# A norm of tokens moved from VectorE to ScalarE, and two differences of h made in one operation

## The chip, the cores and the metric

The kernel runs on one core of a Trainium2 chip. The metric is device microseconds of one execution: the median of three runs before the change, and the same after it. Lower is better.

## The reference

Two layers are applied twice to x of 2048 tokens by 576 features. `_A_ref` is attention with 32 heads of 18, each token looking at 8 keys at distance 0, 2, ..., 14; `_B_ref` is a feed-forward part of width 4608 with SiLU. Each gets a normalised x (mean and variance over the 576 features, no weights).

```python
def _layernorm(x, axis=-1, eps=1e-5):
    m = jnp.mean(x, axis=axis, keepdims=True)
    v = jnp.var(x, axis=axis, keepdims=True)
    return (x - m) / jnp.sqrt(v + eps)
...
    def _B_ref(x, w1, w2):
        h = jnp.einsum("bsd,df->bsf", x, w1)
        h = _silu(h)
        out = jnp.einsum("bsf,fd->bsd", h, w2)
        return out

    x = A_x
    x = x + _A_ref(_layernorm(x, axis=-1), A_wqkv, A_wo)
    x = x + _B_ref(_layernorm(x, axis=-1), B_w1, B_w2)
    x = x + _A_ref(_layernorm(x, axis=-1), A_wqkv, A_wo)
    x = x + _B_ref(_layernorm(x, axis=-1), B_w1, B_w2)
    return x
```

## The kernel before

Everything is float32 in and out; a factor of a matrix product is split into two float16 parts (a high one, and the rest), and three products of parts stand for one. The tokens are taken in chunks of 512 (four tiles of 128 tokens, `NJ`), four chunks for each of the two rounds, so that there are eight steps s = 0 to 7. A step is: attention (`attention`), projection (`project`), norm, feed-forward. Attention runs on VectorE (products, sums, softmax) after a qkv product on TensorE; the feed-forward is nearly all TensorE.

In steps 0 and 1 the feed-forward is done plainly (`ffn`). From step 2 on it is done by block products (`ffn_pairs`): the four 2x2 blocks of a product are made from seven products P1 to P7 of sums and differences of blocks. The forms of the tokens are made in `forms`, called once for each of the steps 2 to 7. It takes the mean and variance of each of the four tiles (bn_stats, lines 1162 and 1163), an inverse square root by Newton's method for all four (`newton`, lines 530 to 539, thirteen small operations on 128x4), then normalises each tile by one VectorE operation that subtracts the mean and multiplies (line 1179), and makes four differences for each of the two halves a of the tokens (line 1184). Each of the seven forms is then split into a high part (ScalarE, line 1193) and a low part (VectorE, line 1198) and turned by a DMA transpose that SP issues (line 1203) into a tile xf, of which there are nine. These are the right sides of the products of line 1232. In steps 2 and 3 the normalised tiles go into areas of their own (`home`), in steps 4 to 7 they are written over x.

Of the feed-forward's other side, the pairs q = 0 to 17 of each step: seven products into PSUM banks, ScalarE copies (`snap`, line 1236), VectorE additions (line 1239), SiLU on ScalarE (lines 1256 to 1261). In steps 6 and 7 (`TWICE`) the second product is by block products too, and `hidden_forms` makes three more forms of h from rows of a tile hq with seven rows of 128x256: row 4 = 6 + 3, row 5 = 4 - 0, row 2 = 1 - 5, row 6 = 0 - 6 (line 1286), and then splits rows 0 to 2 and 3 to 6 into high and low parts (ScalarE line 1291, VectorE line 1294). `seconds` multiplies them (line 1322) and adds the result to x (line 1331). In steps 2 to 5 the second product is line 1345, and line 1353 takes its five banks out.

The order of the work is not written out by hand. Each operation is handed to a planner (`Plan`) by `op`, with an engine, an estimated duration, the keys it reads and writes, and a priority. `Plan.order` plays time forward: whenever an engine is free in its model, the ready operation of lowest priority number and then of lowest number in the program starts, if its buffers are free. The result is one list, and each engine, and each queue that issues DMAs, works through its part of it strictly in that order on the chip. The planner looks at nothing that lies ahead of its clock. The estimates are in the code: 2.55 us for `newton`, 0.58 for a normalisation, 0.42 for a difference of h. ScalarE's table loads are modelled for operations that name a table (exp, silu).

Of the kernel before, what the change touches and what calls it, by code (L numbers as in the profile page):

```python
# [13 lines left out]
AF = mybir.ActivationFunctionType  # L14
ALU = mybir.AluOpType
AX = mybir.AxisListType

P = 128
# [8 lines left out]
NJ = 4  # L27
# [17 lines left out]
LNX = 512.0  # L45
# [29 lines left out]
class Plan:  # L75
# [18 lines left out]
    def op(self, eng, dur, fn, reads=(), writes=(), prio=0.0, nbytes=0, table=None, after=(), lanes=1, lag=0.0):  # L94
        o = Op()
        o.lag = lag
        o.eng, o.dur, o.fn, o.prio, o.seq, o.nbytes, o.table = eng, dur, fn, prio, len(self.ops), nbytes, table
        o.outs, o.end, o.lanes = [], None, lanes
        deps = set(after)
        for k in reads:  # L100
            if k in self.writer:
                deps.add(self.writer[k])
        for k in writes:
            if k in self.writer:
                deps.add(self.writer[k])
            deps.update(self.readers.get(k, ()))
        for k in reads:
            self.readers.setdefault(k, []).append(o)
        for k in writes:
            self.writer[k] = o  # L110
            self.readers[k] = []
        deps.discard(o)
        o.deps = deps
        o.n = len(deps)
        for d in deps:
            d.outs.append(o)
        o.bufs = []
        for k in (*reads, *writes):
            b = k[0] if isinstance(k, tuple) else k
            if isinstance(b, Buf) and b not in o.bufs:  # L120
                o.bufs.append(b)
                b.left += 1
                if b.turn is None:
                    b.turn = self.named[b.tag]
                    self.named[b.tag] += 1
        self.ops.append(o)
        return o
# [152 lines left out]
def sliding_attention_silu_ffn(ctx: ExitStack, tc: tile.TileContext, x, wqkv, wo, w1, w2, out):  # L280
    nc = tc.nc
# [5 lines left out]
    op = S.op  # L287
# [11 lines left out]
    def T(b):  # L299
        if isinstance(b, tuple):  # L300
            return T(b[0])[:, b[1]]
        return S.tags[b.tag][b.slot]
# [221 lines left out]
    def newton(st, mv, nt, on_act, unit, js=slice(0, NJ)):  # L524

        v, r, a, b = (T(nt)[:, i, js] for i in (0, 1, 3, 4))
        if on_act == 2:
            nc.vector.tensor_scalar(v, T(st)[:, js, 0, 1], 1.0 / D, EPS, op0=ALU.mult, op1=ALU.add)
        else:
            nc.vector.tensor_scalar(v, T(mv)[:, js, 1], EPS, None, op0=ALU.add)  # L530
        nc.vector.tensor_scalar(a.bitcast(I32), v.bitcast(I32), 1, None, op0=ALU.logical_shift_right)
        nc.vector.tensor_scalar(r.bitcast(I32), a.bitcast(I32), -1, 0x5F3759DF, op0=ALU.mult, op1=ALU.add)
        for s in (1.0, unit):

            nc.vector.tensor_tensor(a, r, r, op=ALU.mult)
            nc.vector.tensor_tensor(a, a, v, op=ALU.mult)
            nc.vector.tensor_scalar(b, a, 0.375 * s, -1.25 * s, op0=ALU.mult, op1=ALU.add)
            nc.vector.tensor_tensor(b, b, a, op=ALU.mult)
            nc.vector.scalar_tensor_tensor(r, b, 1.875 * s, r, op0=ALU.add, op1=ALU.mult)
        if on_act in (1, 3):  # L540
            nc.vector.tensor_scalar(T(nt)[:, 2, js], T(mv)[:, js, 0], -1.0, None, op0=ALU.mult)

# [613 lines left out]
    def forms(xs, prio, home=None, late=(), into=None):  # L1156

        st, mv, nt = Buf("st"), Buf("mv"), Buf("nt")
        for j in range(NJ):
            def stats(j=j):  # L1160
                for h in range(2):
                    nc.vector.bn_stats(T(st)[:, j, h, :], T(xs[j])[:, h * KH:(h + 1) * KH])
                nc.vector.bn_aggr(T(mv)[:, j, :], T(st)[:, j])
            op("DVE", 0.99, stats, [xs[j]], [(st, j), (mv, j)], prio)
        op("DVE", 2.55, lambda: newton(st, mv, nt, False, LNX), [(st, j) for j in range(NJ)] + [(mv, j) for j in range(NJ)], [nt], prio)
        out, ys = {}, [Buf(home[0]), Buf(home[1])] if home else [Buf(into)] * 2

        def view(a, r):
            if home:
                return T(ys[a])[:, r]  # L1170
            if r > 3:
                return T(ys[a])[:, a, r - 4]
            return T(xs[a + 2 - r // 2 * 2])[:, r % 2 * KH:(r % 2 + 1) * KH]

        def key(a, r):
            return (ys[a], r) if home else (ys[a], a, r) if r > 3 else xs[a + 2 - r // 2 * 2]
        for a in range(2):
            for j, r in ((a + 2, 0), (a, 2)):
                op("DVE", 0.58, lambda a=a, j=j, r=r: nc.vector.tensor_scalar(
                    T(ys[a])[:, r:r + 2, :].rearrange("p a b -> p (a b)") if home else T(xs[j]), T(xs[j]), T(mv)[:, j, 0:1], T(nt)[:, 1, j:j + 1],  # L1180
                    op0=ALU.subtract, op1=ALU.mult), [xs[j], (mv, j), nt], [key(a, r), key(a, r + 1)], prio)

            for o, u, v in ((4, 0, 2), (5, 1, 4), (6, 1, 0), (7, 3, 5)):
                op("DVE", 0.45, lambda a=a, o=o, u=u, v=v: nc.vector.tensor_tensor(view(a, o), view(a, u), view(a, v), op=ALU.subtract),
                   [key(a, u), key(a, v)], [key(a, o)], prio, after=late)
        for n in P_ORDER:
            r, x = Y_ROW[n], Buf("xf")
            for a in range(2):
                f = Buf("yf")

                def hi(f=f, a=a, r=r):
                    d, y = T(f), view(a, r)
                    nc.scalar.activation(d[:, 0:KH], y, AF.Copy)
                    nc.scalar.activation(d[:, KH:KH + 32], y[:, 2 * P:KH], AF.Copy)

                def lo(f=f, a=a, r=r):
                    d, y = T(f), view(a, r)
                    nc.vector.tensor_tensor(d[:, 3 * P:KB], y[:, 0:2 * P], d[:, 0:2 * P], op=ALU.subtract)
                    nc.vector.tensor_tensor(d[:, KH + 32:3 * P].rearrange("p (a b) -> p a b", a=2), y[:, None, 2 * P:KH].to_broadcast([P, 2, 32]),
                                            d[:, None, 2 * P:KH].to_broadcast([P, 2, 32]), op=ALU.subtract)  # L1200
                op("ACT", 0.65, hi, [key(a, r)], [(f, 0)] if home else [(f, 0), (x, "hold", a)], prio)
                done = op("DVE", 0.64, lo, [key(a, r), (f, 0)], [(f, 1)], prio)
                op("SP", 1.34, lambda f=f, a=a, x=x: nc.sync.dma_start_transpose(T(x)[:, :, a * P:(a + 1) * P], T(f)),
                   [(f, 0), (f, 1)], [(x, a)], prio, nbytes=P * KB * 4)
            out[n] = x
        formed.append(done)
        return out

    def ffn_pairs(s, xf, xs, first):
# [3 lines left out]
        for g, n in enumerate(G2):  # L1213
# [4 lines left out]
            for q in range(q0, q0 + n):  # L1218
# [44 lines left out]
                if twice:  # L1263
                    hidden_forms(q, hq, h, pd)
                    continue
# [16 lines left out]

    def hidden_forms(q, hq, h, pd):

        for r, u, v, o in ((4, 6, 3, ALU.add), (5, 4, 0, ALU.subtract), (2, 1, 5, ALU.subtract), (6, 0, 6, ALU.subtract)):
            op("DVE", 0.42, lambda hq=hq, r=r, u=u, v=v, o=o: nc.vector.tensor_tensor(T(hq)[:, r], T(hq)[:, u], T(hq)[:, v], op=o),
               [(hq, u), (hq, v)], [(hq, r)], pd - 0.01)
        for r0, r1, sh in ((0, 3, shx), (3, 7, shy)):
            sc = sh[:, q:q + 1]
            m = (r1 - r0) * 2 * P  # L1290
            op("ACT", 0.3 + m / 1200, lambda hq=hq, h=h, sc=sc, r0=r0, r1=r1: nc.scalar.activation(
                flat_rows(T(h)[:, 0, r0:r1]), flat_rows(T(hq)[:, r0:r1]), AF.Copy, scale=sc),
               [(hq, r) for r in range(r0, r1)] + ["wsc"], [(h, r0)], pd)
            op("DVE", 0.22 + m / 960, lambda hq=hq, h=h, sc=sc, r0=r0, r1=r1: nc.vector.scalar_tensor_tensor(
                flat_rows(T(h)[:, 1, r0:r1]), flat_rows(T(hq)[:, r0:r1]), sc, flat_rows(T(h)[:, 0, r0:r1]),
                op0=ALU.mult, op1=ALU.subtract), [(hq, r) for r in range(r0, r1)] + [(h, r0)], [(h, r0)], pd)

    def flat_rows(t):
        return t.rearrange("p a b -> p (a b)")
# [217 lines left out]
    def turn(s):  # L1517
        XT[s] = forms(load_x(s, s - 1.0, spilt=True), s - 1.0, into="ye")
        X[s] = load_x(s, s - 1.0, spilt=True)
# [73 lines left out]
```

## Time and profile before

| | us |
|---|---|
| median of three runs | 2123.3 (2121.58 to 2124.65) |
| the profiled execution, as a run | 2119.38 |
| its span, first to last instruction | 2117.6 |
| TensorE busy | 2088.3 |
| VectorE busy | 1754.9 |
| ScalarE busy | 1025.8 |
| GpSimd busy | 388.5 |

The mean granted TensorE clock is 0.998 of full. The profile gives instructions by line of the kernel, by engine and by the program's tile names (buffer numbers left out); tiles that share an area carry the area's name, so hq appears as `wq` or `w`, and the forms' tiles as `wos`, `o`, `prs` and `x`. A matmul's end is modelled, and since matmuls are pipelined the shown durations of neighbours overlap: what one really takes is read from the starts, or from a piece of many. "Idle before" is the time that an engine sat still before an instruction, with the instruction that ended the wait.

### The profile page before, as it was taken

To read this page: it belongs to the slowest core of one execution; us is meant where nothing else is said; L and a number is where in the kernel's file an instruction comes from. 1 tells how busy PE (TensorE), PEld (TensorE's weight loads), DVE (VectorE), ACT (ScalarE), POOL (GpSimd) and SP (SyncE) were. 2 spreads that over 40 slices of the span, in tenths; PEclk is the share of its full clock that TensorE was granted. 3 is DMA by queue.
4 is the path that set the end of the run, shared out by engine and by line. 5 is a ranking of instruction groups with operands and counts; after the bars stand their busy time and mean duration, and the time that the engine had idled before them with its cause. 6 is when DMAs were issued, how large, how long until landed. Compare 5 with 4: busy or idle time off the path is not lost.

```text
span 2117.6 us, 41751 instructions
## 1 busy us (share of the span) xinstructions
PE 2088.3 (99%) x16017; PEld 1539.5 (73%) x16017; DVE 1754.9 (83%) x2861; ACT 1025.8 (48%) x1857; POOL 388.5 (18%) x628
## 2 busy tenths in 40 slices
PE   8999999999999999999999999999999999999999
PEld 4556556665566888877786777777788888888887
DVE  8899999999876998679997978986996748766665
ACT  7555787644345454434434433434444545444442
POOL 2133566343322232011111001001000000000000
PEclk9999999999999999999999999999999999999999
DMA  6477777687989889886677896786989999779772
GB/s 188 146 212 256 236 258 248 214 243 221 250 206 297 264 275 252 210 261 189 177 220 208 218 273 195 217 225 185 247 256 302 330 258 290 218 213 272 221 210 76
DMA packets 377632, 489.07 MB, mean 231 GB/s; under 512 B 150600, under 2 KB 300724, under 8 KB 373080
## 3 DMA queue, kind: packets, MB, share of 16 engines
q1 hardware_dynamic: 332456, 336.85, 56.9%
q0 software_dynamic: 42960, 148.45, 21.8%
q8 instruction: 125, 2.05, 0.4%
q10 hardware_dynamic: 2016, 1.11, 0.2%
q14 instruction: 75, 0.61, 0.1%
HBM read 350.96 MB, written 86.85 MB: 207 GB/s over the span
## 4 chain that ended last, share of the span: by engine, by line
PE 87%; DVE 6%; DMA 4%; ACT 1%; issue 1%; SPq 0%; POOL 0%; ACTq 0%; DVEq 0%
PE acc L1345 19%; PE z L1232 16%; PE misc L1232 10%; PE z L735 9%; PE acc L1322 9%; PE z L1385 7%; PE acc L1409 4%; PE misc L1345 4%; PE misc L735 3%; PE z L925 3%; PE misc L1385 2%; PE misc L925 1%; DMA kvs<-kvs 1%; DMA yo<-yh 1%; DVE prs L837 1%
## 5 line engine op out<-in xcount | busy, mean ns | idle before, releaser
L1232 PEld LDWEIGHTS <-w 128*128 128x128 f16 x5292 | 516.5, 98 | 74.5 <-issue 2.5
L1345 PE MATMUL acc<-w,h 128*128 128x320 f16 (+2 forms) x3780 | 548.2, 280 | 2.3 <-DVE x L1353 2.3
L1345 PEld LDWEIGHTS <-h 128*128 128x128 f16 x4320 | 407.6, 98 | 122.3 <-issue 3.3
L1232 PE MATMUL z<-xb,w 128*128 128x256 f16 x3213 | 405.0, 273 | 0.5 <-DVE wq L1239 0.5
L1232 PE MATMUL misc<-xb,w 128*128 128x256 f16 x2079 | 272.2, 273 | 1.1 <-DVE wq L1239 0.8
L735 PEld LDWEIGHTS <-xa 128*128 128x128 f16 x1344 | 130.8, 98 | 115.5 <-issue 6.7
L837 DVE TENSOR_TENSOR prs<-qts,kvs 128x2304 f32<-128x2304 f32 x64 | 163.4, 2554 | 18.8 <-DMA kvs<-kvs 17.0
L870 DVE TENSOR_TENSOR prs<-kvs,pe 128x1152 f32<-128x1152 f32 x128 | 170.3, 1352 | 1.0
L841 DVE TENSOR_REDUCE lg<-prs 128x128 f32<-128x2304 f32 x64 | 163.1, 2548 | 0.9
L735 PE MATMUL z<-wq,xa 128*128 128x432 f16 x840 | 160.2, 346 | 2.1 <-ACT h L748 2.1
L1345 PE MATMUL misc<-w,h 128*128 128x384 f16 x540 | 139.7, 326 | 0.0
L877 DVE TENSOR_TENSOR prs<-prs 128x1152 f32<-128x1152 f32 (+1 forms) x128 | 135.1, 1056 | 3.2
L1331 DVE SCALAR_TENSOR_TENSOR x<-acc,d2x,x 128x576 f32<-128x576 f32 (+1 forms) x85 | 68.7, 810 | 57.2 <-PE acc L1322 56.6
L1385 PEld LDWEIGHTS <-w 128*128 128x128 f16 x588 | 57.9, 99 | 74.2 <-issue 7.6
L1409 PE MATMUL acc<-w,h 128*128 128x288 f16 x864 | 108.4, 286 | 1.9 <-DVE h L1392 1.1
L1409 PEld LDWEIGHTS <-h 128*128 128x128 f16 x864 | 83.7, 98 | 25.2 <-DVE h L1392 1.4
L1385 PE MATMUL z<-xb,w 128*128 128x512 f16 x420 | 93.9, 379 | 0.7 <-DVE w L1011 0.6
L1385 PE MATMUL z<-xb,wq 128*128 128x512 f16 x420 | 92.8, 379 | 1.7 <-ACT h L1387 1.7
L1236 ACT ACTIVATE wq<-z 128x256 f32<-128x256 f32 x107 | 40.8, 382 | 103.8 <-PE z L1232 103.7
L1387 ACT ACTIVATE h<-z,d 128x512 f32<-128x512 f32 x60 | 40.9, 682 | 94.9 <-PE z L1385 86.4
L1322 PEld LDWEIGHTS <-h 128*128 128x128 f16 x756 | 74.0, 98 | 17.6
L925 PEld LDWEIGHTS <-yo 128*128 128x128 f16 x672 | 65.7, 98 | 18.6 <-issue 1.9
(322 smaller groups left out, 3369.0 us busy)
## 6 DMA issues: line engine op xcount, KB each, us to landing
w<-wfs SPq DMA_DIRECT2D x756, 160.0 KB, 3.9
w<-w2s SPq DMA_DIRECT2D x180, 288.0 KB, 4.9
wq<-wqs SPq DMA_DIRECT2D x17, 1080.0 KB, 6.6
kvs<-kd POOLq DMA_DIRECT2D x8, 1584.0 KB, 8.4
w<-w1s SPq DMA_DIRECT2D x36, 320.0 KB, 5.9
wfs<-xa POOLq DMA_DIRECT2D x18, 640.0 KB, 4.6
kvs<-wts SPq DMA_DIRECT2D x80, 144.0 KB, 3.1
w2s<-w POOLq DMA_DIRECT2D x36, 288.0 KB, 4.7
```

The lines of the kernel that those rows point to most:

```text
L735: nc.tensor.matmul(T(m)[:, :3 * UC], a, b, start=n == 0, stop=n == len(pl) - 1)
L837: nc.vector.tensor_tensor(T(pr), T(qt)[:, j:j + 2, None, :].to_broadcast([P, 2, W, UC]), win(T(kv), j, 2), op=ALU.mult)
L841: nc.vector.tensor_reduce(T(lg)[:, j:j + 2].rearrange("p a w h -> p (a w h)"), T(pr).rearrange("p a w (h d) -> p (a w h) d", d=DH), axis=A ...
L870: nc.vector.tensor_tensor(T(pr)[:, a].rearrange("p w (h d) -> p w h d", d=DH), v, T(pe)[:, j + a, :, :, None].to_broadcast([P, W, UH, DH]) ...
L877: nc.vector.tensor_tensor(t[:, :, 0:h, :], t[:, :, 0:h, :], t[:, :, h:2 * h, :], op=ALU.add)
L925: nc.tensor.matmul(T(m)[:, 0:288], a, b, start=n == 0, stop=n == len(pl) - 1)
L1232: nc.tensor.matmul(t, w[:, u, :], v[:, r, :], start=first and m == 0, stop=m == 6, skip_group_check=True)
L1322: nc.tensor.matmul(T(acc)[:, j, 0:KH], T(hb[t])[:, a, row[k], j * P:(j + 1) * P], T(wb[k, t])[:, w, :], start=k in (5, 1, 2) and t == 0 an ...
L1331: nc.vector.scalar_tensor_tensor(v, T(acc)[:, a:b, 0:KH], d2x[:, g:g + 1], v, op0=ALU.mult, op1=ALU.add)
L1345: nc.tensor.matmul(T(fa[b])[:, o:o + 2 * n].rearrange("p (a b) -> p a b", a=2), h(f, a, j), w(f)[:, :, v, c:c + n], start=q == f == m == 0 ...
L1385: nc.tensor.matmul(T(z), v, u, start=m == 0, stop=m == len(pl) - 1)
L1409: nc.tensor.matmul(T(acc)[:, h, 0:288], T(hb[q])[:, a, j * P:(j + 1) * P], T(wbs[q][0])[:, h, w, :], start=q == 0 and m == 0, stop=q == n ...
```

## The change

In `forms`, the four tiles of a step are normalised by ScalarE instead of VectorE: x * r + (-mean * r), an Identity activation with scale and bias read per token. `newton` gets a mode 4 for it, with one more operation that makes -mean * r for the four tiles; the planner's estimate for `newton` stays at 2.55 us, and the normalisation is handed to it as 0.7 us of ScalarE. In `hidden_forms`, rows 5 and 6 are made by one VectorE operation over two rows: its first operand steps backwards from row 4 to row 0, its second forwards from row 0 to row 6. Four operations become three, in the order 4, (5 and 6), 2.

```diff
@@ newton
+        if on_act == 4:
+            nc.vector.scalar_tensor_tensor(T(nt)[:, 2, js], T(mv)[:, js, 0], -1.0, r, op0=ALU.mult, op1=ALU.mult)
         if on_act in (1, 3):
             nc.vector.tensor_scalar(T(nt)[:, 2, js], T(mv)[:, js, 0], -1.0, None, op0=ALU.mult)
@@ forms
-        op("DVE", 2.55, lambda: newton(st, mv, nt, False, LNX), [(st, j) for j in range(NJ)] + [(mv, j) for j in range(NJ)], [nt], prio)
+        op("DVE", 2.55, lambda: newton(st, mv, nt, 4, LNX), [(st, j) for j in range(NJ)] + [(mv, j) for j in range(NJ)], [nt], prio)
@@ forms
-                op("DVE", 0.58, lambda a=a, j=j, r=r: nc.vector.tensor_scalar(
-                    T(ys[a])[:, r:r + 2, :].rearrange("p a b -> p (a b)") if home else T(xs[j]), T(xs[j]), T(mv)[:, j, 0:1], T(nt)[:, 1, j:j + 1],
-                    op0=ALU.subtract, op1=ALU.mult), [xs[j], (mv, j), nt], [key(a, r), key(a, r + 1)], prio)
+                op("ACT", 0.7, lambda a=a, j=j, r=r: nc.scalar.activation(
+                    T(ys[a])[:, r:r + 2, :].rearrange("p a b -> p (a b)") if home else T(xs[j]), T(xs[j]), AF.Identity,
+                    bias=T(nt)[:, 2, j:j + 1], scale=T(nt)[:, 1, j:j + 1]), [xs[j], (mv, j), nt], [key(a, r), key(a, r + 1)], prio)
@@ hidden_forms
-        for r, u, v, o in ((4, 6, 3, ALU.add), (5, 4, 0, ALU.subtract), (2, 1, 5, ALU.subtract), (6, 0, 6, ALU.subtract)):
-            op("DVE", 0.42, lambda hq=hq, r=r, u=u, v=v, o=o: nc.vector.tensor_tensor(T(hq)[:, r], T(hq)[:, u], T(hq)[:, v], op=o),
-               [(hq, u), (hq, v)], [(hq, r)], pd - 0.01)
+        op("DVE", 0.42, lambda: nc.vector.tensor_tensor(T(hq)[:, 4], T(hq)[:, 6], T(hq)[:, 3], op=ALU.add),
+           [(hq, 6), (hq, 3)], [(hq, 4)], pd - 0.01)
+
+        def differences():
+            t = T(hq)
+            first = bass.AP(tensor=t.tensor, offset=t[:, 4].offset, ap=[t.ap[0], [-4 * 2 * P, 2], [1, 2 * P]])
+            nc.vector.tensor_tensor(t[:, 5:7], first, t[:, 0:7:6], op=ALU.subtract)
+        op("DVE", 0.69, differences, [(hq, 4), (hq, 0), (hq, 6)], [(hq, 5), (hq, 6)], pd - 0.01)
+        op("DVE", 0.42, lambda: nc.vector.tensor_tensor(T(hq)[:, 2], T(hq)[:, 1], T(hq)[:, 5], op=ALU.subtract),
+           [(hq, 1), (hq, 5)], [(hq, 2)], pd - 0.01)
```

## Rows read from the trace of the kernel before

**Rows 1.** The page's first part: the span, and for each engine its busy us, share of the span and instructions.
```profile
span 2117.6 us, 41751 instructions
PE 2088.3 (99%) x16017; PEld 1539.5 (73%) x16017; DVE 1754.9 (83%) x2861; ACT 1025.8 (48%) x1857; POOL 388.5 (18%) x628
```

**Rows 2.** Busy time in stretches of the span: start:end, length, then busy us and instructions of PE, PEld, DVE, ACT and POOL, the granted clock, the DMA share and GB/s.
```profile
0.00:606.70 606.70, 587.16 (x3782) 357.14 (x3783) 564.64 (x929) 365.09 (x628) 227.46 (x368) 0.99 0.73 224
606.70:900.00 293.30, 292.84 (x2350) 225.32 (x2349) 237.45 (x404) 140.21 (x259) 76.10 (x112) 1.00 0.91 255
900.00:1557.00 657.00, 652.80 (x5099) 491.25 (x5098) 570.24 (x820) 266.03 (x515) 68.80 (x118) 1.00 0.78 217
1557.00:1740.00 183.00, 182.43 (x1565) 150.08 (x1564) 122.31 (x239) 84.50 (x148) 12.89 (x24) 1.00 0.97 294
1740.00:2113.50 373.50, 373.08 (x3229) 315.67 (x3227) 259.27 (x471) 169.96 (x310) 3.23 (x6) 1.00 0.75 218
2113.50:2117.60 4.10, 0.04 (x1) 0.00 (x0) 0.94 (x2) 0.00 (x0) 0.00 (x0) 0.86 0.31 109
```

**Rows 3.** Who PE waited for, from 606.7 us to the end: us in total, times, longest.
```profile
PE acc L1345 <- DVE x L1353: 2.3, 5, 0.7
PE misc L925 <- DVE wq L1239: 1.8, 1, 1.8
PE misc L1232 <- DVE wq L1239: 0.8, 2, 0.5
PE z L1232 <- DVE wq L1239: 0.5, 1, 0.5
```

**Rows 4.** The chain that ended last, in order of time: start us, us, what (pieces of one kind merged, xcount).
```profile
1551.43 3.06 PE z L1232 x28
...
1706.71 4.41 PE acc L1345 x36
```

**Rows 5.** Instructions of single lines: duration in ns (min/median/max), first and last start, form.
```profile
L1179 DVE TENSOR_SCALAR x<-x,mv,nt x16: 570/574/579, 1122.7 to 1805.7; 128x576 f32<-128x576 f32 x16
...
L539 DVE SCALAR_TENSOR_TENSOR nt<-nt x34: 161/162/165, 8.7 to 1791.7; 128x4 f32<-128x4 f32 x30, 128x2 f32<-128x2 f32 x4
...
L591 ACT ACTIVATE yo<-x,nt x14: 757/767/776, 12.1 to 420.8; 128x576 f32<-128x576 f32 x14
...
L594 ACT ACTIVATE yh<-yo,nt x14: 758/775/777, 12.9 to 424.7; 128x576 f16<-128x576 f32 x14
...
L1291 ACT ACTIVATE h<-wq,shy x12: 1132/1148/1149, 1741.1 to 2049.6; 128x1024 f16<-128x1024 f32 x12
...
L1286 DVE TENSOR_TENSOR wq<-wq x96: 372/424/427, 1738.9 to 2083.8; 128x256 f32<-128x256 f32 x96
...
L1083 DVE TENSOR_TENSOR wq<-wq x72: 548/552/560, 435.9 to 835.5; 128x384 f32<-128x384 f32 x72
...
L1331 DVE SCALAR_TENSOR_TENSOR x<-acc,d2x,x x85: 509/818/821, 1760.6 to 2114.0; 128x576 f32<-128x576 f32 x83, 128x288 f32<-128x288 f32 x2
```

**Rows 6.** Instructions in order of time in step 2's norm and up to its first product: start us, us, engine, line, operation, tiles.
```profile
606.77 0.58 DVE L1179 TENSOR_SCALAR o<-x,mv,nt 128x576 f32<-128x576 f32 x1
...
617.42 2.54 SPq L1203 DMA_TRANSPOSE xb<-yh  x2
...
663.78 0.93 PE L1232 MATMUL misc<-xb,w 128*128 128x256 f16 x7
```

**Rows 7.** The same for step 4's norm, which lies in an attention stage; in brackets the idle time before an instruction and what ended it.
```profile
1120.58 0.16 DVE L539 SCALAR_TENSOR_TENSOR nt<-nt 128x4 f32<-128x4 f32 x1
...
1127.97 0.46 DVE L1184 TENSOR_TENSOR wos<-x,x 128x288 f32<-128x288 f32 x1
...
1128.47 0.44 ACT L1193 ACTIVATE yh<-wos 128x288 f16<-128x288 f32 x1 [0.61 <-DVE wos L1184]
...
1134.89 2.56 DVE L837 TENSOR_TENSOR prs<-qts,kvs 128x2304 f32<-128x2304 f32 x1 [2.42 <-DMA kvs<-kvs]
...
1145.61 0.93 PE L1232 MATMUL misc<-xb,w 128*128 128x256 f16 x7 [0.48 <-DVE wq L1239]
```

**Rows 8.** The same around PE's longest wait after 606.7 us.
```profile
1264.80 0.25 PE L1345 MATMUL acc<-w,h 128*128 128x192 f16 x1
...
1266.83 1.88 PE L925 MATMUL misc<-wos,yo 128*128 128x288 f16 x14 [1.79 <-DVE wq L1239]
```

**Rows 9.** The same for the last pair of step 7.
```profile
2091.50 1.09 DVE L1286 TENSOR_TENSOR w<-w 128x256 f32<-128x256 f32 x3
...
2095.66 1.01 DVE L1294 SCALAR_TENSOR_TENSOR xa<-w,shx,xa 128x768 f16<-128x768 f32 x1
...
2099.29 0.71 PEld L1322 LDWEIGHTS <-xa 128*128 128x128 f16 x6
```

**Rows 10.** Around PE's longest wait before 606.7 us: two stretches as in rows 2, and three pieces of the chain.
```profile
577.00:580.00 3.00, 0.56 (x2) 0.25 (x2) 1.56 (x4) 0.00 (x0) 0.00 (x0) 0.51 1.12 157
580.00:585.00 5.00, 5.00 (x17) 1.91 (x15) 4.83 (x14) 1.85 (x3) 0.00 (x0) 0.61 0.26 79
...
562.23 16.19 DMA yo<-yh
...
579.44 5.36 PE misc L1385 x14
588.24 3.02 PE misc L1385 x14
```

## The prediction

> **What bounds the kernel now.** I began with the page's first part: TensorE is busy 99% of the span, VectorE 83%, ScalarE 48% [rows 1]. Two of these are high enough to set the pace, so the next view is busy time by stretch. I cut the span at 606.7 us, for a reason in the code: the planner never looks ahead of its clock, and the first operation that the change touches is step 2's normalisation, which starts at 606.77 us [rows 6]. Up to there both kernels get the same lists; whatever PE loses before (606.70 - 587.16 = 19.5 us [rows 2]) stays. Behind the cut, up to PE's last matmul near 2113.5, PE is idle 0.46 + 4.20 + 0.57 + 0.42 = 5.65 us of 1506.8 [rows 2], and 4.1 us at the end are the last addition and the way out. The waits say on whom: on VectorE alone, nine times, 5.4 us together [rows 3]. A modelled end hides part of each wait: around the longest, PE's starts lie 2.03 us apart; 192 columns at one per cycle of 2.4 GHz are 0.08 us of it and 1.79 is reported [rows 8], so 0.16 us more for each of nine, 1.5 us. So 7.2 us (an estimate from these rows) is all that this change can give back, if PE is at its pace between the waits.
>
> Whether it is must be asked, since busy time of pipelined matmuls can be padded. The chain has pieces of one kind: 28 matmuls of 256 columns in 3.06 us, 109 ns each, and 36 of 288 columns in 4.41 us, 122.5 ns each [rows 4]. One column per cycle at the granted 2.4 GHz level is 106.7 and 120 ns. PE runs within some 2% of its columns, and these 2% are per matmul, whose number the change leaves alone.
>
> The Trainium skill (Perfetto Trace Analysis, "Identifying the Most-Contended Engine") says that matmul busy time is no measure of how near the limit TensorE is, and to look at weight loads' busy share instead. That share is 73% here [rows 1], which by this rule leaves room on TensorE and would make VectorE the engine to relieve. The starts in rows 4 disagree for this kernel.
>
> **The change, part by part.**
>
> Norm, VectorE's side: six calls of `forms` with four tiles make 24 operations of 0.575 us [rows 5], 13.8 us gone. Six operations on 128x4 come in, 0.162 each [rows 5], 1.0 us. Net 12.8 us.
>
> Norm, ScalarE's side: 24 activations of 128x576. No row has an activation with both scale and bias read per token. The nearest, same size with one of the two, take 0.767 and 0.775 [rows 5]; the ends are 0.44 (288 elements [rows 7]) and 1.15 (1024 elements [rows 5]). I take 0.77: 18.5 us, between 10.6 and 27.6. Behind the cut ScalarE is busy 140.2 + 266.0 + 84.5 + 170.0 = 660.7 of 1506.8 us [rows 2], so it has room for either end.
> The Trainium skill (ScalarE: Activation LUTs, "What ACT_TABLE_LOAD costs") gives 186 ns plus 0.833 per element plus 93 for each per-token operand, which would make 0.85 us, 20.4 in all; rows with one operand agree (0.76 by it). The sum above would be 2 us longer on an engine with 846 us to spare.
>
> Norm, the chain: from the end of `newton` to the first difference two tiles are needed. Before, 2 x 0.575 = 1.15. After, 0.16 + 2 x 0.77 = 1.7, and two crossings of engines, 0.04 each (a difference ends at 1127.97 + 0.46 = 1128.43, ScalarE starts on it at 1128.47 [rows 7]). The first form is 0.6 us later per call. Cover: step 2's first transpose is issued at 617.42 and its first product runs at 663.78 [rows 6], 46 us behind; PE meanwhile has step 1's work. Without that cover the six calls would cost 6 x 0.6 = 3.6 us. The planner isn't told of the 0.16 us operation, so each norm stands at ScalarE's head up to 0.2 us earlier than VectorE is ready. Behind it are copies out of product banks; the products take 7 x 109 ns = 0.77 us each and three banks turn, so 0.2 us reaches nobody.
>
> Differences of h: 36 pairs of steps 6 and 7. Two operations of 0.424 become one over 512 elements. From 256 to 384 elements the duration grows by 0.128 us (0.424 to 0.552 [rows 5]), so 512 should take 0.68; the ends are 0.552 (384 elements) and 0.818 (576, one operand from PSUM) [rows 5]. I take 0.68, 0.17 saved each, 6.1 us of VectorE in all, between 1.1 and 10.7. The stage in which it lies has PE idle for 0.42 of 373.5 us [rows 2]. Even the last pair is ready early: three differences start at 2091.50, VectorE is done with the low parts at 2096.67, and PE loads the first of these weights at 2099.29 [rows 9], 2.6 us later. Worth nothing in time.
>
> The sum: VectorE is freed of 12.8 + 6.1 = 18.9 us of its 1189 us behind the cut (237.45 + 570.24 + 122.31 + 259.27 [rows 2]), 1.6%. On the path that sets the end lie only PE's 7.2 us of waits. By share of load 1.6% of these go, 0.1 us. By place: the wait that follows a norm in VectorE's queue is that at 1145.61, 0.48 us [rows 7]; but between them VectorE sat still for 2.42 us until keys landed (1134.89 [rows 7]), which swallows the 2 us gained at the norm. The longest, 1.79 us at 1266.83 [rows 8], stands in the middle of attention. New orders behind the cut will remove some waits and make others. I put the gain at 0.4 us: 2119.38 - 0.4 = 2119.0 for an execution like the profiled one. The median shown is 2123.3, 3.9 above it, so the forecast is 2122.9.
>
> **The rivals.**
>
> VectorE sets the pace, and what it is freed of shows in the time: 2122.9 + 0.4 - 18.9 = 2104.4. For it: all of PE's waits are on VectorE, and attention holds it at 570 of 657 us [rows 2]. Against: rows 4. This is also where the skill's rule on busy shares would lead.
>
> The waits vanish: a VectorE that runs a little ahead of the plan is never late for a bank. At best 2123.3 - 7.2 = 2116.1. To be more than 0.2% faster (4.2 us, about what a measurement here can tell from no change) six tenths of the waits have to go.
>
> ScalarE is held up (the slow side). Its queue is strict. A norm at its head waits for `newton`, and `newton` can be late by one attention operation, 2.56 us [rows 7]. Behind the norm stand the copies out of PE's banks. PE has about two products of cover, 2 x 0.77 = 1.5 us; past that point it stops. Price: 2.56 - 1.5 = 1.1 us per call, six calls 6.4 us: 2129.7. It decides only where the delay exceeds 1.5 us. For it: the norms of steps 4 to 6 lie in attention. Against: ScalarE is idle over half of the time there, and before the change VectorE's waits on ScalarE cost PE nothing in rows 3.
>
> A new order of SP's queue makes one transpose late. Before the cut there is such a place: a transpose that took 16.19 us, after which PE was busy 0.56 of 3 us with the granted clock at 0.51 (the 1.2 GHz level), and the next 14 matmuls took 5.36 us where the same piece later takes 3.02 [rows 10]. One more like it: 2.4 + 2.3 = 4.8 us, 2128.1. For it: DMA is at 0.91 and 0.97 of its engines around the seams [rows 2]. Against: none of PE's waits behind the cut is of this size.
>
> The paired operation saves nothing (its first operand steps backwards and costs 0.85): no difference in the time.
>
> **How the numbers follow.** No change in the time, with or without the pair's saving: 0.60. Waits vanish: 0.12. VectorE sets the pace: 0.03. ScalarE held up: 0.16. A late transpose, or more than one: 0.09. Forecast 2122.9. Faster by over 0.2%: 0.12 + 0.03 = 0.15; slower: 0.16 + 0.09 = 0.25; within: 0.60. The range runs from 2116.8, most of the way to the floor of the waits, to 2130.0, just past the two slow cases; the unknown durations don't widen it, as both engines have room for their ends.
>
> **What would show it.** VectorE's busy time about 19 us lower, ScalarE's 18 to 20 higher, PE's the same to a few us with 16017 matmuls. The new activation near 0.77, the paired difference near 0.68. PE's idle time between 606.7 us and its last matmul between 4 and 9 us, still on VectorE. Where ScalarE is held up, PE waits on ScalarE's line 1236 or 1259 or its followers right behind a norm. I am wrong if PE's busy time falls with VectorE's, or if PE's waits behind the cut double.

## The result, and the profile after

The change made the kernel slower: 2140.46 us (median of five runs, 2137.44 to 2142.81) against 2121.58 us for the kernel before beside it (five runs, the three shown ahead among them, 2116.62 to 2124.65), a ratio of 1.0092 with an interval of 1.0071 to 1.0112, so 18.9 us more in the medians. The forecast was 2122.9 and its range ended at 2130.0. The profiled execution of the changed kernel took 2137.44 us, its span is 18.1 us longer than that of before.

The page's first part of the changed kernel, as in [rows 1]:

```profile
span 2135.7 us, 41728 instructions
PE 2095.6 (98%) x16017; PEld 1541.6 (72%) x16017; DVE 1740.4 (81%) x2807; ACT 1043.3 (49%) x1881; POOL 389.5 (18%) x628
```

VectorE is 14.5 us less busy, ScalarE 17.5 us more: the work moved as the change says. PE (TensorE) has the same 16017 matmuls and is busy 7.3 us longer in a span that is 18.1 us longer. Busy time by stretch, cut as in [rows 2]:

```profile
0.00:606.70 606.70, 586.91 (x3761) 355.81 (x3762) 562.48 (x916) 364.84 (x628) 227.43 (x368) 0.99 0.73 224
606.70:900.00 293.30, 288.13 (x2286) 219.74 (x2285) 230.19 (x396) 141.67 (x257) 76.16 (x112) 0.99 0.91 249
900.00:1557.00 657.00, 646.90 (x5025) 484.81 (x5023) 552.76 (x803) 266.65 (x518) 69.75 (x118) 0.99 0.79 215
1557.00:1740.00 183.00, 183.00 (x1577) 151.23 (x1575) 130.73 (x240) 91.77 (x153) 11.85 (x22) 1.00 0.92 288
1740.00:2113.50 373.50, 372.54 (x3233) 315.78 (x3231) 255.58 (x443) 178.34 (x328) 4.33 (x8) 1.00 0.79 228
2113.50:2135.70 22.20, 18.09 (x148) 14.21 (x146) 8.62 (x12) 0.00 (x0) 0.00 (x0) 1.00 0.16 54
```

Up to the cut PE is as busy as before (586.91 against 587.16 us). Behind it PE is idle 5.17 us where it was 0.46, and 10.10 where it was 4.20; the next two stretches are nearly as before, and the last holds the work that came late. The stretches are fixed in time and the work moved by up to 18 us between them, so a difference of the other engines from row to row is no measure of the change. Whom PE waited for behind the cut, as in [rows 3]:

```profile
PE z L1234 <- DVE wq L1241: 6.4, 2, 6.1
PE z L1394 <- ACT h L1396: 4.1, 1, 4.1
PE acc L1354 <- DVE x L1362: 2.6, 4, 1.2
PE misc L737 <- DVE wq L1241: 1.9, 1, 1.9
PE z L1234 <- DVE yo L1241: 0.6, 1, 0.6
```

Three waits are new: 6.1, 4.1 and 1.9 us. The longest before was 1.8. None of the three names a new instruction, so each is followed back through the queue of the engine that it names.

**Near 639 us**, ScalarE's queue, then PE, then SP's queue (start, us, instruction, and in brackets how long the engine sat idle before it and what released it):

```profile
626.40 0.44 ACT L1195 ACTIVATE yh<-o 128x288 f16<-128x288 f32 x1 [6.27 <-DMA xb<-yh]
635.75 0.44 ACT L1195 ACTIVATE yh<-prs 128x288 f16<-128x288 f32 x1 [8.79 <-DMA xb<-yh]
638.75 0.44 ACT L1195 ACTIVATE yo<-o 128x288 f16<-128x288 f32 x1 [2.44 <-DMA xb<-yo]
641.51 0.44 ACT L1195 ACTIVATE yo<-prs 128x288 f16<-128x288 f32 x1 [2.20 <-DMA xb<-yo]
642.88 0.67 ACT L1396 ACTIVATE h<-z,d 128x512 f32<-128x512 f32 x1
...
643.60 1.01 PE L1394 MATMUL z<-xb,w 128*128 128x512 f16 x2 [4.13 <-ACT h L1396]
...
622.74 6.94 SPq L1205 DMA_TRANSPOSE xb<-yo  x2
629.78 8.28 SPq L1205 DMA_TRANSPOSE xb<-yh  x2
639.85 3.96 SPq L1205 DMA_TRANSPOSE xb<-yo  x2
```

Read from the bottom: the transposes of step 2's forms hold SP's queue for two to four us each. A form's high part (line 1195) can't be written until a transpose has released its buffer, so ScalarE sits idle with a high part at its head for 6.3, 8.8, 2.4 and 2.2 us. Behind these stands the SiLU of step 1 that empties the product bank PE needs. Its product is long done; it runs at 642.88, and PE stands still for 4.1 us.

**Near 1041 us**, VectorE's queue, then PE, then SP's:

```profile
1039.17 0.46 DVE L590 TENSOR_SCALAR yh<-x 128x576 f16<-128x576 f32 x1 [8.11 <-DMA xa<-yh]
...
1046.87 0.42 DVE L1241 TENSOR_TENSOR wq<-misc,wq 128x256 f32<-128x256 f32 x1
...
1048.01 1.65 PE L1234 MATMUL z<-xb,w 128*128 128x256 f16 x7 [6.14 <-DVE wq L1241]
...
1031.31 6.22 SPq L509 DMA_TRANSPOSE xa<-yh  x1
```

The same with another engine: a float16 split of the next attention chunk's norm (line 590) waits 8.11 us for a buffer that a transpose holds, 6.22 us of it in SP's queue; behind it in VectorE's queue stand seven us of other work and the additions that empty PE's banks. In the kernel before, the transposes of this chunk are hardly quicker (two in 9.29 us, here 3.54 and 6.22), but VectorE has over 9 us of other work in front of the next split, which then finds its buffer free; PE is busy for all of the 7 us from 1041 to 1048 there:

```profile
1020.49 9.29 SPq L509 DMA_TRANSPOSE xa<-yh  x2
...
1032.19 0.45 DVE L588 TENSOR_SCALAR yh<-x 128x576 f16<-128x576 f32 x1
```

**Near 942 us** it happens once more, smaller, and the releaser is a store:

```profile
941.47 0.46 DVE L590 TENSOR_SCALAR yh<-x 128x576 f16<-128x576 f32 x1 [4.78 <-DMA xn<-yh]
...
944.37 2.72 PE L737 MATMUL misc<-wq,xa 128*128 128x432 f16 x14 [1.91 <-DVE wq L1241]
```

Each long stop costs more than its wait. The stretches from the stop and behind it (columns as in [rows 2]; the granted clock is the third number from the end), and two pieces of the chain of one kind:

```profile
639.00:643.60 4.60, 0.47 (x4) 0.10 (x1) 2.14 (x7) 2.37 (x10) 0.00 (x0) 0.79 0.79 107
643.60:650.00 6.40, 6.40 (x22) 2.67 (x22) 6.40 (x13) 6.33 (x11) 0.82 (x2) 0.61 0.85 237
1041.00:1048.00 7.00, 0.86 (x8) 0.52 (x6) 6.86 (x13) 0.34 (x1) 0.00 (x0) 0.75 1.19 275
1048.00:1052.00 4.00, 4.00 (x21) 2.68 (x21) 3.90 (x5) 2.40 (x4) 0.00 (x0) 0.59 1.09 344
...
643.60 5.61 PE z L1394 x14
...
655.09 3.02 PE misc L1394 x14
```

After the first stop PE runs at a mean clock of 0.61, between the 1.2 GHz level (0.5) and full speed, for 6.4 us and 14 products take 5.61 us instead of 3.02, so 2.6 us more; after the second it runs 4.0 us at 0.59, 1.6 us lost (4.0 x 0.41, an estimate). The three places sum to 4.1 + 2.6 + 6.1 + 1.6 + 1.9 = 16.3 us. The wait near 575 us, which lies before the cut where both lists are the same, took 7.3 us in this execution and 4.4 in that of before (3.7 to 7.3 in the other runs). At the cut 2.6 us of that are left: the same product starts at 609.58 us instead of 607.02. They are not the change's doing. Less the 1.8 us of [rows 8], which are gone, that is 16.3 + 2.6 - 1.8 = 17.1 of the 18.1 us.

The new instructions themselves, by line (count, busy us, mean ns of one, idle before):

```profile
L1181 ACT ACTIVATE x<-x,nt 128x576 f32<-128x576 f32 x16 | 12.9, 855 | 4.4 <-DVE nt L541 3.4 <-DMA kvs<-w2s 1.0
L541 DVE SCALAR_TENSOR_TENSOR nt<-mv,nt 128x4 f32<-128x4 f32 x6 | 1.0, 162 | 0.2
L1293 DVE TENSOR_TENSOR wq<-wq 128x512 f32<-128x512 f32 x24 | 16.6, 692 | 0.8
```

### The profile page after: what moved, and what is told of

Same layout as the page of the kernel before. It is cut to its first block, busy times and chain, and to the rows that moved or that the text cites. A ratio compares the mean times of both kernels' runs of the same rounds, so it can differ in the third digit from the quotient of the medians.

```text
span 2135.7 us, 41728 instructions
## 1 busy us (share of the span) xinstructions
PE 2095.6 (98%) x16017; PEld 1541.6 (72%) x16017; DVE 1740.4 (81%) x2807; ACT 1043.3 (49%) x1881; POOL 389.5 (18%) x628
## 4 chain that ended last, share of the span: by engine, by line
PE 83%; DVE 8%; DMA 5%; issue 1%; ACT 1%; SPq 0%; DVEq 0%; ACTq 0%; POOL 0%; POOLq 0%
PE acc L1354 19%; PE z L1234 15%; PE misc L1234 10%; PE acc L1331 9%; PE z L737 8%; PE z L1394 6%; PE acc L1418 4%; PE misc L1354 4%; PE misc L737 3%; PE z L927 3%; PE misc L1394 2%; PE misc L927 1%; DVE prs L839 1%; DMA yo<-yh 1%; DVE lg L843 1%
## 5 line engine op out<-in xcount | busy, mean ns | idle before, releaser
L737 PE MATMUL z<-wq,xa 128*128 128x432 f16 x770 | 147.4, 346 | 1.7 <-ACT h L750 1.5
L737 PE MATMUL misc<-wq,xa 128*128 128x432 f16 x406 | 80.4, 351 | 6.8 <-ACT qts L807 4.0
```

What stands on the lines that cost most here:

```text
L737: nc.tensor.matmul(T(m)[:, :3 * UC], a, b, start=n == 0, stop=n == len(pl) - 1)
```

## The experiments

**The order or the instructions.** The change does two things: other instructions, and, since the planner is told other engines and durations, another order of everything behind 606.7 us. Theory: the order costs the time. Rival: the instructions do. The first run keeps the new instructions but hands them to the planner as the old ones:

```diff
-                op("ACT", 0.7, lambda a=a, j=j, r=r: nc.scalar.activation(
+                op("DVE", 0.58, lambda a=a, j=j, r=r: nc.scalar.activation(
...
+        def form(r, u, v, o):
+            if r == 5:
+                differences()
+            elif r != 6:
+                nc.vector.tensor_tensor(T(hq)[:, r], T(hq)[:, u], T(hq)[:, v], op=o)
...
```

> The changed kernel's instructions (activation for the norm, the extra operation of newton, the paired difference) in the order of the kernel before: the planner is told of the old operations, so PE's, SP's and GpSimd's lists are those of before, row by row. Theory 'order' (the 18.9 us come from new orders behind 606.7 us, which put instructions that wait for a late transpose in front of those that empty PE's banks): no difference from the kernel before, 2118 to 2125 us, no wait of PE over 3 us behind 606.7, VectorE's busy time near 1740 and ScalarE's near 1043 as in the changed kernel. Rival 'instruction' (0.85 us activations that wait for newton at ScalarE's head hold up the copies out of PE's banks, or the forms come later): 2135 to 2142, as the changed kernel.

2121.93 us, ratio 1.0008 (0.9999 to 1.0017). The second hands the old instructions to the planner as the new ones:

```diff
-                op("DVE", 0.58, lambda a=a, j=j, r=r: nc.vector.tensor_scalar(
+                op("ACT", 0.7, lambda a=a, j=j, r=r: nc.vector.tensor_scalar(
...
+        def differences():
+            nc.vector.tensor_tensor(T(hq)[:, 5], T(hq)[:, 4], T(hq)[:, 0], op=ALU.subtract)
+            nc.vector.tensor_tensor(T(hq)[:, 6], T(hq)[:, 0], T(hq)[:, 6], op=ALU.subtract)
...
```

> The old kernel's instructions in the order of the changed kernel: the planner is told of the activations and of the paired operation, but VectorE subtracts and multiplies, newton has no extra operation and the pair is two operations. Theory 'order': 2135 to 2142 us, with the waits of PE near 639 us (about 4 us, on ScalarE's SiLU copy) and near 1041 us (about 6 us, on VectorE's additions). Rival 'instruction': 2118 to 2125 us and neither wait.

2139.86 us, ratio 1.0089 (1.0076 to 1.0103). Its two longest waits of PE behind the cut are those of the changed kernel (lines shifted by two or three):

```profile
PE z L1232 <- DVE wq L1239: 6.5, 2, 6.1
PE z L1391 <- ACT h L1393: 4.7, 1, 4.7
```

In the traces, PE's and SP's instructions follow one another in the first run as in the kernel before, and in the second as in the changed one. Both runs say the same with one half of the change each: the order costs the time, and the new instructions make no difference clear of noise (between 0.2 us gained and 3.6 us lost, by the first run's interval).

**The two halves.** The norm's half alone, then the pair's half alone, with instructions and planner as in the change (the diff shown ahead, with the other half left as before):

> The norm's half of the change alone, planner and instructions; the differences of h as before. Its lists are those of the changed kernel up to the last two steps. Theory 'order': all the large waits of the changed kernel lie in front of these steps, so 2134 to 2142 us. Rival 'pair' (the operation that steps backwards, or the lists that it changes in steps 6 and 7, cost the time): 2120 to 2128 us.

> The pair's half of the change alone: its lists differ from those of before only from about 1700 us on, where VectorE has room. Theory 'order': 2117 to 2126 us, no difference, since VectorE is not what PE waits for in steps 6 and 7. Rival 'pair': 2130 us or more. Were VectorE's 6 us worth anything there, 2115.

The norm's half took 2141.30 us, ratio 1.0093 (1.0077 to 1.0109); the pair's half 2121.03, ratio 0.9999 (0.9990 to 1.0008). The loss is the norm's alone. The pair's new order begins only near the end of the span.

**Is it the head of the queue?** In the changed kernel's list, after planning, single operations are moved behind a later one, together with what depends on them or shares a buffer with them; PE's list stays as it was. Each move names the operations by their place in the list. First near 639 us, five high parts behind one SiLU and its copy:

```diff
+    split, silu = [L[n] for n in (1700, 1702, 1706, 1712, 1715)], L[1722]
+    behind(L, split, silu)
```

> The changed kernel with its plan, but one SiLU of step 1's feed-forward and its copy (they empty the product bank that PE waits for at 639 us) stand in ScalarE's queue ahead of five forms' high parts instead of behind them; PE's list is unchanged. Theory 'queue head' (high parts that wait for late transposes hold up the SiLU behind them): PE's wait of 4.1 us goes, and the 2.4 us at the lower clock after it: 2140.5 - 6.5 = 2134.0, between 2131 and 2137. Rival 'load' (PE is late there because the transposes are slow, whatever stands in front): the wait comes up at another instruction, 2138 to 2143.

No gain: 2140.55 us, ratio 1.0097 (1.0077 to 1.0116). The SiLU ran at 630.36 instead of 642.88, but PE stopped from 639.9 us on, about where it had stopped before, now for a low part of h on VectorE, and then again:

```profile
643.89 0.34 PE L1354 MATMUL misc<-w,h 128*128 128x384 f16 x1 [4.01 <-DVE h L1401]
...
647.06 0.50 PE L1354 MATMUL misc<-w,h 128*128 128x384 f16 x1 [2.75 <-ACT h L1398]
```

Next near 1041 us, two splits behind three additions, and then both moves together:

```diff
+    halves, add = [L[n] for n in (2986, 3009)], L[3017]
+    behind(L, halves, add)
```

> The changed kernel with its plan, but two float16 splits of the next attention chunk's norm stand in VectorE's queue behind the three additions that empty PE's banks, instead of ahead of them; PE's list is unchanged. Theory 'queue head': PE's wait of 6.1 us near 1041 goes, and 1.8 us at the lower clock after it: 2140.5 - 8.1 = 2132.4, between 2129 and 2136. Rival 'load': the splits' transposes come later, and PE waits for them at the qkv product instead: 2138 to 2143.

> Both moves together in the changed kernel's plan, two places in two queues, nothing else. Theory 'queue head': 2140.5 - 6.5 - 8.1 = 2125.9, between 2122 and 2130, which leaves some 4 us to the kernel before, spread over small waits. Rival 'load': 2137 to 2143.

The additions' move alone gave 2130.97 us, ratio 1.0047 (1.0029 to 1.0066), 9.5 us back where 8.1 were expected. Its VectorE does the additions as PE's products end, and then the splits, without a wait:

```profile
1041.21 0.42 DVE L1241 TENSOR_TENSOR wq<-misc,wq 128x256 f32<-128x256 f32 x1 [0.76 <-PE misc L1234]
...
1042.95 0.45 DVE L590 TENSOR_SCALAR yh<-x 128x576 f16<-128x576 f32 x1
```

Both together gave 2134.96, ratio 1.0070 (1.0054 to 1.0085), not 2125.9, and no better than the additions' move alone. So near 1041 us the head of the queue is the cause, shown; near 639 us moving one SiLU does not help. Two more tries there, with the additions' move kept: the forms' splits spread between step 1's SiLUs, copies and low parts of h, and then the last two of them two SiLUs further back.

```diff
+    order = [([1733, 1741], 1753), ([1712, 1715], 1753), ([1706], 1742), ([1702], 1737), ([1700], 1724)]
...
+    order = [([1733, 1741], 1775), ([1712, 1715], 1753), ([1706], 1742), ([1702], 1737), ([1700], 1724)]
```

> As the run with both moves, but around 639 us the high and low parts of five forms are spread between step 1's SiLUs, copies and low parts of h in ScalarE's and VectorE's queues, each behind the work that PE needs first, instead of all standing in front or all behind one SiLU; PE's list is unchanged. Theory 'queue head' (the move of one SiLU failed because h's low parts still stood behind the forms' low parts in VectorE's queue, where PE's 4.0 us wait appeared): 2131.0 (with the additions moved alone) - 6.5 = 2124.5, between 2121 and 2128. Rival 'load' (the transposes are too slow there for any order): waits move on once more, 2130 to 2137.

> As the interleaved run, but the last two of the forms' splits around 650 us, behind which PE's wait of 4.2 us appeared there, stand behind two more SiLUs of step 1. Theory 'queue head': the wait near 656 us goes and none over 2 us takes its place before 900 us: 2131.0 - 6.5 = 2124.5, between 2121 and 2128. Rival 'load': the wait moves on to the first block products, which need these transposes, or elsewhere: 2130 to 2137.

2132.93 us, ratio 1.0051 (1.0034 to 1.0068), and 2136.12, ratio 1.0080 (1.0060 to 1.0101): no better than the additions' move alone. The wait moved on, first to a SiLU near 656 us, then to the first block products near 678 us, which wait for the transposes themselves. The longest wait behind the cut in the one, and in the other:

```profile
PE misc L1394 <- ACT h L1396: 4.2, 1, 4.2
```

```profile
PE z L1234 <- DMA xb<-yh: 5.2, 1, 5.2
```

**What slows the transposes near 639 us.** GpSimd loads weights beside them, in the kernel before up to 623.9 us, in the changed one up to 629.0. In the changed kernel's list the second chunk of these loads is moved behind the stores that follow:

```diff
+    behind(L, [L[1713]], L[1753])
```

> The changed kernel's plan, but one chunk of weights that GpSimd loads from about 621 to 629 us beside the forms' transposes is loaded some 20 us later, behind the stores that follow; the other queues keep their order (one group of four products on VectorE moves with it). If the transposes are slow (8 of them held SP's queue from 617 to 644 us) because of this load, they take under 2.5 us each and PE's wait near 639 us shrinks by 2 us or more: 2131 to 2138. If they are slow by themselves: the wait stays at 4 us, 2138 to 2143.

2137.32 us, ratio 1.0075 (1.0057 to 1.0093). The medians are 3.1 us apart, but this interval overlaps with the changed kernel's (1.0071 to 1.0112), so the gain in time is not clear of noise; what the load does is read from the trace. The SP queue of this run:

```profile
617.90 1.25 SPq L1205 DMA_TRANSPOSE xb<-yh  x1
...
622.13 7.03 SPq L1205 DMA_TRANSPOSE xb<-yo  x2
629.26 3.31 SPq L1205 DMA_TRANSPOSE xb<-yh  x2
632.67 2.54 SPq L1205 DMA_TRANSPOSE xb<-yo  x2
```

The same eight transposes end at 635.2 instead of 643.8, the last four in 5.9 us instead of 12.2 (8.28 + 3.96), and the SiLU behind them runs at 634.57. The 4.1 us wait is gone; 2.7 us came back as small waits up to 682 us. So this load slows the last four transposes, and with them the SiLU.

It is not all that slows them. Under 2.5 us each was expected without the load, and the pair ahead of these four took 7.03 us without it as it took 6.94 with it. In the kernel before, two pairs beside the same loads are quick: 2.54 us [rows 6], and

```profile
620.07 2.57 SPq L1203 DMA_TRANSPOSE xb<-yo  x2
```

What makes the first slow pair slow stays open. With three orders of ScalarE's and VectorE's queues that moved the wait and won nothing, the place near 639 us is explained in part only.

**Do the places add up?** This move, the two splits near 1041 us, and one split near 942 us behind two additions:

```diff
+    halves, add = [L[n] for n in (2986, 3009)], L[3017]
+    halves2, add2, weights, h_low = L[2720], L[2734], L[1713], L[1753]
+    behind(L, halves, add)
+    behind(L, [halves2], add2)
+    behind(L, [weights], h_low)
```

> The changed kernel's plan with three places mended and nothing else: GpSimd's load of one chunk of weights behind the stores that follow (as in the run with the load alone), the two splits near 1041 us behind the additions (as in the run with the additions alone), and one more split of the same kind near 939 us, which waits 5.0 us for its buffer, behind two additions that PE waits 2.1 us for. If the change's cost is the sum of such places: 2140.5 - 3.1 - 9.5 - 2.1 = 2125.8, between 2122 and 2129. If they are not independent (each mended place makes another late): 2129 to 2135.

2125.82 us, ratio 1.0021 (1.0010 to 1.0031): with three places in the order mended, 14.6 of the 18.9 us are back, and the sum of the places holds. That it came out at the forecast's 2125.8 is luck: the eleven runs lie between 2122.11 and 2132.26 us, one of the three terms (3.1) is within the noise, and another (2.1) was read from a wait and not from a run of its own. The rest, 4.6 us above the kernel before beside it, was not taken apart; the profiled execution, the longest of the eleven, still has waits of 2.7, 2.1 and 2.0 us.

**Would any new order cost this?** The kernel before with its own instructions, where only one estimate of the planner is changed, by 0.02 us up or down:

```diff
-                op("DVE", 0.58, lambda a=a, j=j, r=r: nc.vector.tensor_scalar(
+                op("DVE", 0.60, lambda a=a, j=j, r=r: nc.vector.tensor_scalar(
...
+                op("DVE", 0.56, lambda a=a, j=j, r=r: nc.vector.tensor_scalar(
```

> The kernel before, every instruction as it was, but the planner is told 0.60 us for a norm of forms instead of 0.58; its lists differ from those of before from 614 us on, about as much as the changed kernel's do. If any new order costs about as much as the change's, 2130 to 2145; if the change's order is an unlucky one among many that are alike, 2118 to 2125; if orders scatter, anything between, with waits of PE of several us at places of their own.

> The kernel before, every instruction as it was, with the planner told 0.56 us for a norm of forms instead of 0.58; PE's list differs from that of before only in its last part, from about 1400 us on, VectorE's and SP's from about 1250. If what costs time is any new order, 2130 to 2142; if it is the orders around 639 and 1041 us, which stay as they were here, 2117 to 2125.

With 0.60 it took 2140.70 us, ratio 1.0096 (1.0078 to 1.0115); with 0.56, 2119.49, ratio 0.9995 (0.9985 to 1.0004). Then the changed kernel with the measured durations of the new instructions, and both kernels with transposes declared twice as dear:

```diff
+        op("DVE", 2.75, lambda: newton(st, mv, nt, 4, LNX), [(st, j) for j in range(NJ)] + [(mv, j) for j in range(NJ)], [nt], prio)
...
+                op("ACT", 0.85, lambda a=a, j=j, r=r: nc.scalar.activation(
...
+        return op("SP", 1.34 * (1 + (prio > 1.5)), lambda: nc.sync.dma_start_transpose(dst(), fl(T(src))), [(src, 0), (src, 1)], [(key, j)], prio,
...
+                op("SP", 2.68, lambda f=f, a=a, x=x: nc.sync.dma_start_transpose(T(x)[:, :, a * P:(a + 1) * P], T(f)),
```

> The changed kernel, with the planner told the measured durations of the new instructions: 0.85 us for a norm on ScalarE instead of 0.70, 2.75 for newton instead of 2.55. If wrong estimates of the new instructions make the bad order, 2117 to 2125. If the order is bad because of what the planner believes of transposes, or only by accident, it need not improve: 2125 to 2145, with waits of PE of 3 us and more at places of its own.

> The changed kernel, with the planner told twice the cost of a transpose of forms and of the later chunks' norms (2.68 us in SP's queue and twice the bytes). If the planner's belief that a transpose is quick is what puts waiting instructions in front, 2116 to 2128, without a wait of PE over 3 us behind 606.7. Rival 'accident' (any new order can have such places): anything up to 2145.

> The kernel before, with the planner told twice the cost of the same transposes; all instructions are the old ones. If transposes believed quick are the cause: 2114 to 2124. Rival 'accident': the order before is a good one among worse, and most other orders cost something: 2125 to 2145.

True durations didn't help: 2141.62 us, ratio 1.0096 (1.0073 to 1.0119). Dear transposes made it far worse: 2187.88, ratio 1.0306 (1.0279 to 1.0332), for the changed kernel, and 2191.45, ratio 1.0321 (1.0298 to 1.0344), for the kernel before. So my theory that the planner goes wrong because it believes transposes quick falls, at least as a repair by one factor. The two slow orders from small edits (0.60, and true durations) stop near 1041 us, at the same place as the changed kernel. VectorE in the run with 0.60, and in the run with true durations:

```profile
1031.78 0.46 DVE L588 TENSOR_SCALAR yh<-x 128x576 f16<-128x576 f32 x1 [10.62 <-DMA xa<-yh]
```

```profile
1036.00 0.46 DVE L590 TENSOR_SCALAR yh<-x 128x576 f16<-128x576 f32 x1 [9.09 <-DMA xa<-yh]
```

Both are followed by a wait of PE of 6.2 us. Among the orders that were run, that of before is a favourable one: those that keep its first half (0.56, the pair alone) cost nothing, and every one of the planner's in which that half differs cost 18 us or more. They are few, and not independent, since three of them share the stop near 1041 us; why the planner comes to it so often is not shown.

## Why the prediction was wrong

Right: PE is the bound, and VectorE's freed time is worth nothing: with all new instructions in the old order the time is the same within the noise, as the forecast said of them. The rival in which VectorE sets the pace falls with it. The Trainium skill (Perfetto Trace Analysis, "Identifying the Most-Contended Engine") names two measures of TensorE's headroom, MFU (matmul work done, as a share of what the peak rate would do) and weight loads' busy share. The prediction took up only the second. By it alone VectorE would have been the engine to relieve, and the run in the old order speaks against that: VectorE is 12.4 us less busy (1742.5 against 1754.9) and nothing is gained. MFU was not worked out here. In the lists the cut at 606.7 us held, and the paired difference took 0.69 us where 0.68 was forecast.

Wrong without effect: the activation took 0.855 us, not 0.77. The Trainium skill's figures (ScalarE: Activation LUTs, "What ACT_TABLE_LOAD costs") had given an estimate of 0.85, and the trace agrees. ScalarE, busy 17.5 us longer, had room for it. VectorE's busy time fell by 14.5 us in the changed kernel, and by 12.4 with the same instructions in the old order, instead of by 18.9. The term that was most too large is the pair's: its half alone freed 2.2 us (VectorE busy 1752.7 against 1754.9), not 6.1. The forecast added up durations of single operations, 0.424 each, but neighbours on VectorE overlap: three of the old differences in a row took 1.09 us [rows 9], 0.36 each, so that leaving one out saves less than its duration.

The step that failed is the last of the sum: "New orders behind the cut will remove some waits and make others. I put the gain at 0.4 us". PE's 7.2 us of waits bound what a new order can give back. They don't bound what it can cost, and the sum has no term for that: the slow side of the range came from two rivals, priced at 6.4 and 4.8 us and taken one at a time. The measured term is a loss of about 19 us, and the two runs that part order from instructions put it on the order.

The rival of the late transpose had most of the mechanism: a transpose that stops PE, with the lower clock behind it, as in [rows 10]. It was priced for one place at 4.8 us, and it came at two places of 6.7 and 7.7 us, with a third of 1.9 behind a store. Its chance was 0.09, held down by "none of PE's waits behind the cut is of this size". That sentence took the old order's waits as evidence on the new one. What it missed as well is the step between transpose and PE: PE doesn't wait for the transposed tile, but for a SiLU or an addition that stands in a strict queue behind an instruction which waits for the transpose's buffer. So a transpose needn't be later than before to cost time; near 1041 us it was the split that had moved ahead. The place of [rows 10] already shows that step. VectorE sat idle for 5.35 us with a split at its head, and the addition that PE waited for stood behind it:

```profile
578.44 0.52 DVE L898 TENSOR_SCALAR yh<-o,so 128x576 f16<-128x576 f32 x1 [5.35 <-DMA yo<-yh]
578.88 0.51 DVE L927 SCALAR_TENSOR_TENSOR x<-misc,so,x 128x288 f32<-128x288 f32 x1
...
579.44 1.01 PE L1385 MATMUL misc<-xb,w 128*128 128x512 f16 x2 [4.39 <-DVE x L927]
```

The rival in which ScalarE is held up named the right engine for the first place and the wrong cause. Norms at ScalarE's head waited 3.4 us for newton's last operation by the profile's count, and the first one of step 2 another 4.8 us, where the forecast had 0.2 us or a single operation's 2.56: the profile names no releaser for it, but it starts at 609.57 us, as that operation ends. The run in the old order has the same 4.8 us, and its time is that of the kernel before within the noise.

My own test "if PE's waits behind the cut double" was the right one to name: 5.4 us became 15.6.

## What to carry to other kernels

Where a planner writes the order, an edit of one engine or one duration is two changes: test the new instructions in the old order first, then the new order with the old instructions, and keep an order that is known to be good while instructions change under it. What the bound engine waits for now says what can be gained, not what a new order can lose; for that, look in each strict queue for instructions that wait for a buffer held by a DMA, and ask what stands behind them.

## What was not expected of the hardware

The same DMA transpose of a form held SP's queue for about 1.25 us or for about 4 us (8.28 for two). Loads beside it are part of that: moving one load of weights out of the way took four transposes from 12.2 to 5.9 us. They are not all of it: in the kernel before four transposes beside such loads took 5.1 us (2.54 and 2.57), and the slow pair of 7 us stayed slow without the load. Bytes moved say little of this, since the slow stretch from 636 to 642 us of the changed kernel moved fewer of them (119 GB/s) than the stretch before its loads ended (218 GB/s from 624 to 630). In a stop of PE of 4 to 6 us the granted clock fell to the 1.2 GHz level (0.51 in [rows 10]; means of 0.61 and 0.59 over the 6.4 and 4.0 us behind the two stops here), which cost 1.6 to 2.6 us more.
